# Two quarters of logits in one visit to TensorE, and reloads moved by one or two half products

## The chip, the cores and the metric

The kernel runs on one core of a Trainium2 chip. TensorE (PE in the profile, PEld its weight loads) multiplies matrices into PSUM. VectorE (DVE), ScalarE (ACT) and GpSimd (POOL) work element by element. The DMAs of this kernel are all issued by SyncE's queue (SP). The metric is the time of one execution on the device in microseconds, median of the runs.

## The reference, cut to what matters

Three layers follow one another: pooled attention (8 batches, 8 heads, 576 positions; keys and values averaged over 8 neighbours), a feed-forward layer on its 4608 tokens, and a soft mixture of experts on the result.

```python
x = attention(q, k, v)                  # 4608 tokens x 512
h = x @ w_in                            # 512 -> 2048, the first layer
g = maximum(h, 0) ** 2                  # 4608 x 2048
x2 = g @ w_out                          # 2048 -> 512
logits = x2 @ phi                       # 512 -> 32 slots
d = exp(logits - logits.max(0));  d /= d.sum(0)
slot_input = d.T @ x2                   # 32 x 512
slot_out = experts(slot_input)          # 8 experts, 512 -> 1024 -> 512
c = exp(logits - logits.max(1));  c /= c.sum(1)
return c @ slot_out
```

The kernel never forms x2. It multiplies w_out by phi once (a matrix A, 2048 x 32, tile `a_sb`) and takes the logits as g @ A. The sum d.T @ x2 is taken as (d.T @ g) @ w_out.

## The kernel before, in words

The tokens are 36 tiles of 128. The columns of h (d_ff, 2048) are four quarters j of 512. One product is one tile by one quarter: 12 matmuls (line 400; xh and xl are the high and the low part of the activations), so 144 products in all. Tiles 0 to 3 go by a list of their own; after that the pairs of tiles (t, t+1) follow one another, quarter by quarter. A slot is half a product, 6 matmuls; a table `ev` says what is issued after which slot, and a scheduler then sets the order on each engine. `issue_after` pins work behind a named instruction: behind the last store, the last square on VectorE, or (new) the last first-layer matmul.

Each product goes through ScalarE (relu, line 412) and VectorE or GpSimd (square, line 418; VectorE reads the product straight from PSUM) and is stored to DRAM (line 422). The product's PSUM tile `l` has two buffers, so product n+2 waits until the square (or relu) of product n has read its own.

The logits of a pair of tiles need g transposed. `reload_turned` (line 447) reads 2 tiles by one quarter back from DRAM with four DMAs of 128 KB, into one of five buffers (tiles `turned` and `tmp`). `g_T` (line 455) transposes it in 32 x 32 blocks on VectorE. `logits` (line 480) then does four matmuls of 32 columns each, side by side in the array, 256 tokens long. Quarters accumulate in the PSUM tile `pl` and ScalarE copies the sum out (line 494). For the early pairs (t below ND = 10, and two late tiles) each quarter has a PSUM tile of its own (`att`, two buffers, shared with the attention); ScalarE copies the first quarter and VectorE adds the other three (line 492).

When all four quarters are there, `log_T` (line 506) spreads the logits, VectorE takes the maximum, ScalarE the exponentials, VectorE transposes them (line 541, tile `d`), and `dg` (line 551) adds d.T @ g to a running sum. Attention of later tiles (lines 188 to 289) runs between the products: on TensorE lines 188, 204 and 281, on ScalarE and VectorE the rest. After the last tile (about 737 us) the experts and the last product follow.

Of the kernel before, what the change touches and what calls it, by code (L numbers as in the profile page):

```python
# [17 lines left out]
def kernel(  # L18
# [12 lines left out]
    nc = tc.nc  # L31
# [9 lines left out]
    NT = NTOK // P  # L41
    NPAIR = H // 2
    KD = DM // P
    NQ = 4
# [4 lines left out]
    SLOTS = 8  # L49
    NI = 4  # L50
    ND = 10
# [41 lines left out]
    def ps(name):  # L93
        return ps2.tile([P, 512], F32, tag=name, name=name)
# [229 lines left out]
    st_t, mark, n_st = {}, {}, [0]  # L324
# [35 lines left out]
    def natural(x):  # L360
        return x.rearrange("p (a c f) -> p c a f", a=4, f=32)
# [25 lines left out]
    hp_t, g_t, gT_t, L_t, dT_t, d_t, sc_d = {}, {}, {}, {}, {}, {}, {}  # L387
    pl_t = {}

    def l1_half(t, j, half):  # L390
        if half == 0:
            hp_t[t, j] = ps("l1")
        xh, xl = x_t[t]
        w = wq[j]
        steps = [
            (x[:, kk], w[:, hl, kk]) for kk in range(KD) for x, hl in ((xh, 0), (xh, 1), (xl, 0))
        ]
        n = len(steps) // 2
        for i in range(half * n, (half + 1) * n):
            nc.tensor.matmul(hp_t[t, j], steps[i][0], steps[i][1], start=(i == 0), stop=(i == 2 * n - 1))  # L400
        if half == 1:
            hp = hp_t.pop((t, j))
            if j == NQ - 1 and ND <= t < NT - 4:
                g = tmp[:, 6 + t % 2]
            elif j == NQ - 2 and t % 2 == 0 and ND <= t < NT - 4:
                g = tmp[:, 4 + t // 2 % 2]
            else:
                g = gp.tile([P, QF], F32, tag="g", name="g")
            r = p2.tile([P, QF], F32, tag="r", name="r")
            sq = "VVVPVPVV"[2 * j + t % 2]  # L410
            last_relu.append(
                nc.scalar.activation(out=r, in_=hp, func=AF.Relu, scale=1.0 / (R * R if sq == "V" else R))  # L412
            )
            dst, src, pre = g, r, hp if sq == "V" else r
            if t >= NT - 4:
                dst = natural(g)
                src, pre = (y.rearrange("p (c a f) -> p c a f", c=4, f=32) for y in (src, pre))
            m = eng[sq].tensor_tensor(out=dst, in0=pre, in1=src, op=ALU.mult)  # L418
            if sq == "V":
                mark["sq"] = m  # L420
            if t < NT - 4:
                mark["store"] = nc.sync.dma_start(out=g_dram[t // 2][j, t % 2 * P:(t % 2 + 1) * P], in_=g)
            if t >= ND:
                g_t[t, j] = g
# [42 lines left out]
    def logits(t, j):  # L467
        gT = gT_t.pop((t, j))
        if (t, j) in gT_at:
            gT_free.append(gT_at.pop((t, j)))  # L470
        alone = t < ND or t in (NT - 4, NT - 2)
        n = P if t >= NT - 4 else 2 * P
        if alone:
            pl = ps("att")[:, :n]
        elif j == 0:
            pl = pl_t[t] = ps1.tile([P, n], F32, tag="pl", name="pl")
        else:
            pl = pl_t[t]
        for c in range(CPQ):
            mark["logits"] = nc.tensor.matmul(  # L480
                pl[32 * c:32 * c + 32],
                a_sb[:, c, 32 * j:32 * j + 32],
                gT[:, c],
                start=(alone or j == 0),
                stop=(alone or j == NQ - 1),
            )
        first = t - t % width(t)
        if first not in L_t:
            L_t[first] = p2.tile([P, 2 * P], F32, tag="plsb", name="plsb")
        dst = L_t[first][:, (t - first) * P:(t - first) * P + n]  # L490
        if alone and j > 0:
            nc.vector.tensor_tensor(out=dst, in0=dst, in1=pl, op=ALU.add)
        elif alone or j == NQ - 1:
            nc.scalar.copy(out=dst, in_=pl)

    run, order = {}, []

    def width(t):
        return 1 if t >= NT - 2 else 2
# [98 lines left out]
    def behind(names, fn, *a):  # L598
        with ExitStack() as es:
            for n in names:  # L600
                es.enter_context(tc.issue_after(mark[n].ins))
            fn(*a)
# [81 lines left out]
    def at(slot, fn, *a):  # L684
        ev.setdefault(slot, []).append((fn, a))
# [5 lines left out]
    def run_slot(s):  # L691
        for fn, a in ev.pop(s, []):
            if fn in (g_T, logits, log_T, d_T, dg) and a[0] >= NT - EP:
                early(fn, *a)
            else:
                fn(*a)
# [3 lines left out]
            fn(*a)  # L700

    def post(t, s0, o, step=4):
        for j in range(NQ):
            at(s0 + step * j + o[1], logits, t, j)
        for j in range(NQ):
            at(s0 + step * j + o[0], pinned, "sq", g_T, t, j)
            at(s0 + step * j + o[2], pinned, "store", reload_turned, t, j)

    def post_end(t, s0, p):
        at(s0 + p[0], log_T, t)  # L710
        at(s0 + p[1], d_T, t)
        at(s0 + p[2], dg, t)
# [34 lines left out]
    for j in range(NQ):  # L747
        s0 = 26 + 12 * j
# [7 lines left out]
        attention(t, a_at[t])  # L756
    for t in range(ND, NT - 2, 2):
        if t < NT - 4:
            post(t, SLOTS * t, (12, 14, 6))
        post_end(t, SLOTS * t, (27, 28, 28))  # L760
    for t in (NT - 4, NT - 2):
        s0 = SLOTS * t
        for i in range(2):
            for j in range(NQ):
                at(s0 + 4 * j + 2 * i + LO, logits, t + i, j)
            for j in range(NQ):
                at(s0 + 4 * j + 2 * i + GO, g_T, t + i, j)
# [8 lines left out]
    for t in range(0, ND, 2):  # L776
        s0 = 96 + 28 * (t // 2)
        at(s0 - 5, reload_g, t)
        post(t, s0, (1, 4, -4), 4)
        post_end(t, s0, (20, 21, 22))  # L780
    for b in range(1, B):
        s0 = a_at[b * S // P]
# [59 lines left out]
    steps = (att_qT, att_sc, att_exp, att_norm, att_aT, att_av)  # L842
# [14 lines left out]
    for u, (t, j) in enumerate(units):  # L857
        for half in range(2):
            l1_half(t, j, half)
            run_slot(2 * u + half)  # L860
        if j == NQ - 1:
            x_t.pop(t)
# [26 lines left out]
    for c in range(CPQ):  # L889
        for j in range(NQ):  # L890
# [4 lines left out]
                start=(c == 0),  # L895
                stop=(c == CPQ - 1),
# [12 lines left out]
    for r in range(NR):  # L909
        ph = [ps("l1") for _ in range(2)]  # L910
        for kk in range(KD):
            for n in range(2):
                for j in range(4):
# [4 lines left out]
                        start=(kk == 0),  # L918
                        stop=(kk == KD - 1),
# [104 lines left out]
```

## Time and profile before

| | |
|---|---|
| runs before | 822.71, 829.86, 825.0 us; median 825.0 |
| the profiled execution | 822.68 us, its span 820.7 us |
| TensorE busy | 762.3 us, 93% of the span |
| VectorE busy | 533.4 us, 65% |
| ScalarE busy | 373.2 us, 45% |
| GpSimd busy | 202.5 us, 25% |
| first logits | about 277 us |
| end of the last product's work | about 737 us |

A row of the profile's timeline has the start in us, the length in us, the engine, the line, the operation, the tile written, the tiles read, and in brackets how long the engine was idle before it and what released it. TensorE's float32 matmuls are recorded as two records each, so four logits matmuls read as x8. Starts, not ends, tell what a matmul costs, since matmuls overlap.

### The profile page before, as it was taken

The page shows a single profiled execution, that of the slowest core. Times are in us where ns is not written, and L with a number is a line of the kernel's source. Part 1 is how long each engine was busy: PE and PEld are TensorE (multiplying, and loading weights), DVE is VectorE, ACT ScalarE, POOL GpSimd, SP SyncE. Part 2 cuts the span into 40 slices and gives each one's busy share as a digit, 9 for nine tenths or more (in the row PEclk, how much of TensorE's full clock was granted, in tenths as well). Part 3 has the DMA queues.
Part 4 walks back from the last instruction along what each step waited for, and adds up shares of the span by engine and source line. Part 5 has one row for each costly group of instructions (what it writes and reads, how often), then busy time and mean ns, then how long its engine had stood idle before and what let it go on. Part 6 is the DMA issues. An engine that isn't in the chain of part 4 may idle for free.

```text
span 820.7 us, 14813 instructions
## 1 busy us (share of the span) xinstructions
PE 762.3 (93%) x5352; PEld 529.7 (65%) x5352; DVE 533.4 (65%) x1033; ACT 373.2 (45%) x1107; POOL 202.5 (25%) x208
## 2 busy tenths in 40 slices
PE   7699899979999999998999999979998999998993
PEld 6577678757677776665666666746665666663552
DVE  5886966577836687688868687876666564424333
ACT  3564456334456563453536464654365433331232
POOL 3433532149624330136024414301000001000000
PEclk8579999999999999999999999989999999999996
DMA  9755742666724885788598788667456424969999
GB/s 277 244 166 153 221 167 103 215 175 225 259 112 146 225 233 160 204 234 211 179 291 216 207 258 215 182 194 217 129 184 198 141 91 150 350 253 315 372 352 313
DMA packets 180856, 175.11 MB, mean 213 GB/s; under 512 B 47152, under 2 KB 138288, under 8 KB 180784
## 3 DMA queue, kind: packets, MB, share of 16 engines
q1 hardware_dynamic: 180784, 174.17, 67.9%
q8 instruction: 43, 0.70, 0.3%
q14 instruction: 29, 0.24, 0.1%
HBM read 126.94 MB, written 47.19 MB: 212 GB/s over the span
## 4 chain that ended last, share of the span: by engine, by line
PE 63%; DVE 15%; DMA 11%; ACT 6%; issue 3%; POOL 1%; SPq 1%; DVEq 0%; ACTq 0%
PE l L400 35%; DMA kv<-in_v_dram 3%; PE misc L551 3%; PE pl L480 3%; PE misc L946 2%; PE gT L281 2%; PE gT L204 2%; PE l L914 2%; PE att L281 2%; ACT aT L254 2%; PE att L204 2%; DVE vp L161 2%; DMA g_back<-g_dram 2%; ACT es L215 1%; PE att L480 1%
## 5 line engine op out<-in xcount | busy, mean ns | idle before, releaser
L400 PE MATMUL l<-w,xh 128*128 128x512 f32 x1152 | 383.5, 413 | 11.7 <-DVE g L418 7.0
L400 PEld LDWEIGHTS l<-w,xh 128*128 128x128 f32 x1152 | 209.4, 191 | 82.0 <-issue 17.7
L400 PE MATMUL l<-w,xl 128*128 128x512 f32 x576 | 230.9, 401 | 0.0
L412 ACT ACTIVATE r<-l 128x512 f32<-128x512 f32 x144 | 86.4, 601 | 185.5 <-PE l L400 168.8
L400 PEld LDWEIGHTS l<-w,xl 128*128 128x128 f32 x576 | 109.4, 190 | 30.1 <-issue 4.7
L418 POOL TENSOR_TENSOR g<-r 128x512 f32<-128x512 f32 x36 | 41.2, 1145 | 298.4 <-ACT r L412 247.4
L254 ACT COPY aT<-turned 32x256 f32<-32x256 f32 (+1 forms) x168 | 67.8, 404 | 33.6 <-DVE turned L263 31.3
L418 DVE TENSOR_TENSOR g<-l,r 128x512 f32<-128x512 f32 x75 | 51.2, 684 | 47.2 <-ACT r L412 40.9
L131 POOL TENSOR_TENSOR kv<-kv 72x512 f32<-72x512 f32 x40 | 53.8, 1348 | 88.0 <-DMA kv<-in_v_dram 59.5
L455 DVE STREAM_TRANSPOSE turned<-turned 128x1024 f32<-128x1024 f32 x39 | 47.7, 1230 | 3.8 <-DMA turned<-g_dram 3.7
L256 DVE COPY aT<-turned 32x256 f32<-32x256 f32 (+1 forms) x120 | 43.7, 365 | 5.0 <-PE gT L281 3.1
L317 POOL TENSOR_TENSOR tmp<-tmp 128x512 f32<-128x512 f32 x21 | 28.6, 1361 | 68.8 <-DVE tmp L314 68.8
L215 ACT ACTIVATE es<-att,mx 128x72 f32<-128x72 f32 x120 | 36.8, 333 | 16.2 <-DVE mx L211 16.0
L215 ACT ACTIVATE es<-gT,mx 128x72 f32<-128x72 f32 x120 | 36.8, 329 | 12.7 <-DVE mx L211 12.6
L350 POOL TENSOR_TENSOR w<-tmp,w 128x512 fp32r<-128x512 f32 x16 | 28.6, 1793 | 38.5 <-ACT w L349 34.2
L418 DVE TENSOR_TENSOR tmp<-l,r 128x512 f32<-128x512 f32 x33 | 22.6, 686 | 21.2 <-ACT r L412 15.1
L551 PE MATMUL misc<-g,d 128*32 128x512 f32 x134 | 25.8, 631 | 7.3 <-DVE d L541 7.3
L455 DVE STREAM_TRANSPOSE tmp<-tmp 128x1024 f32<-128x1024 f32 x25 | 30.7, 1231 | 2.4 <-DMA tmp<-g_dram 2.4
L238 DVE TENSOR_TENSOR es<-es,rs 128x576 f32<-128x576 f32 x36 | 31.6, 878 | 1.0
L307 DVE TENSOR_SCALAR tmp<-tmp 128x512 uint32<-128x512 uint32 x32 | 20.0, 624 | 17.4 <-ACT tmp L306 17.4
L132 POOL TENSOR_TENSOR kv<-kv 72x256 f32<-72x256 f32 x40 | 30.3, 763 | 0.6
L204 PEld LDWEIGHTS gT<-kb,qT 128*128 128x128 f32 (+1 forms) x176 | 23.4, 188 | 8.2 <-issue 5.1
(188 smaller groups left out, 1135.3 us busy)
## 6 DMA issues: line engine op xcount, KB each, us to landing
g_dram<-g SPq DMA_DIRECT2D x95, 256.0 KB
turned<-g_dram SPq DMA_DIRECT2D x156, 128.0 KB
w<-in_moe_w_dram SPq DMA_DIRECT2D x32, 512.0 KB
tmp<-g_dram SPq DMA_DIRECT2D x100, 128.0 KB
w<-in_moe_w_dram SPq DMA_DIRECT2D x6, 2048.0 KB
g_back<-g_dram SPq DMA_DIRECT2D x10, 1024.0 KB
kv<-in_k_dram SPq DMA_DIRECT2D x32, 288.0 KB
kv<-in_v_dram SPq DMA_DIRECT2D x32, 288.0 KB
```

The costliest lines, as they stand in the source:

```text
L131: eng.tensor_tensor(out=x[:, :, 0:4], in0=x[:, :, 0:4], in1=x[:, :, 4:8], op=ALU.add)
L204: nc.tensor.matmul(sc[off:off + n, i * 2 * SP:(i + 1) * 2 * SP], qT[:, pi, off:off + n], kb[b % 2][:, pi].rearrange("p a s -> p (a s)"),)
L215: nc.scalar.activation(out=es[:, e], in_=sv[:, h], func=AF.Exp, bias=mx[:, e:e + 1], accum_out=rsum[:, t % 8, e, 0:1],)
L254: nc.scalar.copy(out=dst, in_=src)
L256: eng[e].tensor_copy(dst, src)
L281: nc.tensor.matmul(px[e * D:(e + 1) * D, i * P + off:i * P + off + n], vp_t[b][:, 2 * i + e], aT[:, 2 * i + e, off:off + n],)
L400: nc.tensor.matmul(hp_t[t, j], steps[i][0], steps[i][1], start=(i == 0), stop=(i == 2 * n - 1))
L412: nc.scalar.activation(out=r, in_=hp, func=AF.Relu, scale=1.0 / (R * R if sq == "V" else R))
L418: m = eng[sq].tensor_tensor(out=dst, in0=pre, in1=src, op=ALU.mult)
L455: nc.vector.transpose(out=gc.rearrange("p (n i) -> p n i", i=32), in_=gc.rearrange("p (n f) -> p n f", f=32))
L480: mark["logits"] = nc.tensor.matmul(pl[32 * c:32 * c + 32], a_sb[:, c, 32 * j:32 * j + 32], gT[:, c], start=(alone or j == 0), stop=(alone ...
L551: mark["dg"] = nc.tensor.matmul(dp[32 * j:32 * j + 32], d[:, u], g if t < NT - 4 else natural(g), start=(u == 0), stop=(u == width(t) - 1),)
```

## The change

Logits of two quarters are issued together (`logits_two`), each pinned behind the latest first-layer matmul. For the early pairs the first two quarters share one PSUM tile `att`, and the last two share another: one copy on ScalarE and one addition on VectorE in place of one copy and three additions. The transposes and reloads of even quarters are moved by two slots more than those of odd ones. In slots from the start of the pair, the transposes of the four quarters were at 12, 16, 20, 24 and are now at 14, 16, 22, 24; the reloads were at 6, 10, 14, 18 and are now at 9, 11, 17, 19; the logits were at 14, 18, 22, 26 and are now at 18 and 26 for two each. For the early pairs: transposes 1, 5, 9, 13, now 4, 6, 12, 14; reloads -4, 0, 4, 8, now 0, 2, 8, 10; logits 4, 8, 12, 16, now 8 and 16.

```diff
-            nc.tensor.matmul(hp_t[t, j], steps[i][0], steps[i][1], start=(i == 0), stop=(i == 2 * n - 1))
+            mark["l1"] = nc.tensor.matmul(hp_t[t, j], steps[i][0], steps[i][1], start=(i == 0), stop=(i == 2 * n - 1))
...
-        alone = t < ND or t in (NT - 4, NT - 2)
+        alone = t in (NT - 4, NT - 2)
+        two = t < ND
...
+        elif two and j % 2 == 0:
+            pl = pl_t[t] = ps("att")[:, :n]
...
-                start=(alone or j == 0),
-                stop=(alone or j == NQ - 1),
+                start=(alone or j == 0 or two and j == 2),
+                stop=(alone or j == NQ - 1 or two and j == 1),
...
-        if alone and j > 0:
+        if alone and j > 0 or two and j == 3:
             nc.vector.tensor_tensor(out=dst, in0=dst, in1=pl, op=ALU.add)
-        elif alone or j == NQ - 1:
+        elif alone or j == NQ - 1 or two and j == 1:
             nc.scalar.copy(out=dst, in_=pl)
+
+    def logits_two(t, j):
+        behind(["l1"], logits, t, j - 1)
+        behind(["l1"], logits, t, j)
...
     def post(t, s0, o, step=4):
+        for j in (1, 3):
+            at(s0 + step * j + o[1], logits_two, t, j)
         for j in range(NQ):
-            at(s0 + step * j + o[1], logits, t, j)
-        for j in range(NQ):
-            at(s0 + step * j + o[0], pinned, "sq", g_T, t, j)
-            at(s0 + step * j + o[2], pinned, "store", reload_turned, t, j)
+            b = s0 + step * j + (0 if j % 2 else 2)
+            at(b + o[0], pinned, "sq", g_T, t, j)
+            at(b + o[2], pinned, "store", reload_turned, t, j)
...
-            post(t, SLOTS * t, (12, 14, 6))
+            post(t, SLOTS * t, (12, 14, 7))
...
-        post(t, s0, (1, 4, -4), 4)
+        post(t, s0, (2, 4, -2), 4)
```

What it does to the order shows at two places. The first is TensorE around products 68 and 69 (`l_3617` and `l_3655` before, `l_3602` and `l_3638` in the change). Before:

```order
L400 MATMUL l_3617<-w_577,xh 128x512 x2
L480 MATMUL att<-turned,a_sb 32x256 x4
L400 MATMUL l_3617<-w_577,xl 128x512
L400 MATMUL l_3617<-w_577,xh 128x512 x2
L400 MATMUL l_3617<-w_577,xl 128x512
L400 MATMUL l_3655<-w_577,xh 128x512 x2
L400 MATMUL l_3655<-w_577,xl 128x512
L400 MATMUL l_3655<-w_577,xh 128x512 x2
L400 MATMUL l_3655<-w_577,xl 128x512
L480 MATMUL pl<-tmp,a_sb 32x256 x4
L400 MATMUL l_3655<-w_577,xh 128x512 x2
```

The same place in the change (line 483 is line 480 of before):

```order
L281 MATMUL gT<-aT,vp 64x128 x8
L400 MATMUL l_3638<-w_577,xh 128x512 x2
L400 MATMUL l_3638<-w_577,xl 128x512
L400 MATMUL l_3638<-w_577,xh 128x512 x2
L400 MATMUL l_3638<-w_577,xl 128x512
L483 MATMUL pl<-turned,a_sb 32x256 x4
L483 MATMUL pl<-tmp,a_sb 32x256 x4
L400 MATMUL l_3638<-w_577,xh 128x512 x2
```

Two groups of four logits matmuls that stood apart now stand together between two halves of a product.

The second place is SyncE's queue around the stores of products 63 to 66 (line 422; `g_dram_104` belongs to an early pair, `g_dram_110` to the pair just computed). Before:

```order
L422 DMA g_dram_110<-tmp 128x512
L447 DMA turned<-g_dram_110 32x8x128 x4
L422 DMA g_dram_110<-tmp 128x512
L447 DMA turned<-g_dram_104 32x8x128 x4
L114 DMA qt<-in_q_dram 128x8x64
L422 DMA g_dram_111<-g 128x512
L447 DMA tmp<-g_dram_110 32x8x128 x4
L124 DMA kv<-in_v_dram 72x2x512 x2
L124 DMA kv<-in_k_dram 72x2x512
L422 DMA g_dram_111<-g 128x512
L447 DMA tmp<-g_dram_104 32x8x128 x4
```

In the change:

```order
L422 DMA g_dram_110<-tmp 128x512
L124 DMA kv<-in_v_dram 72x2x512
L422 DMA g_dram_111<-g 128x512
L447 DMA turned<-g_dram_110 32x8x128 x4
L124 DMA kv<-in_v_dram 72x2x512
L124 DMA kv<-in_k_dram 72x2x512
L422 DMA g_dram_111<-g 128x512
L447 DMA tmp<-g_dram_110 32x8x128 x4
L447 DMA turned<-g_dram_104 32x8x128 x4
L422 DMA g_dram_111<-g 128x512
```

The reloads stand behind later stores, and some stand two in a row.

## Rows read from the trace of the kernel before

**Rows 1.** The page's first part: engine, busy us (share of the span) xinstructions.

```profile
span 820.7 us, 14813 instructions
PE 762.3 (93%) x5352; PEld 529.7 (65%) x5352; DVE 533.4 (65%) x1033; ACT 373.2 (45%) x1107; POOL 202.5 (25%) x208
```

**Rows 2.** Tile pl, matmuls and copies: ns min/median/max, first and last start.

```profile
L480 PE MATMUL pl<-turned,a_sb x216: 378/379/404, 276.9 to 679.0; 128*32 128x256 f32 x108
...
L494 ACT COPY plsb<-pl x13: 254/373/415, 304.2 to 737.6; 128x256 f32<-128x256 f32 x11, 128x128 f32<-128x128 f32 x2
```

**Rows 3.** Windows: us, busy PE PEld DVE ACT POOL, clock, DMA share, GB/s.

```profile
350.00:450.00 100.00, 95.96 (x639) 63.86 (x632) 78.48 (x147) 48.75 (x162) 33.31 (x39) 1.00 0.82 228
...
500.00:550.00 50.00, 44.77 (x287) 28.98 (x280) 38.36 (x82) 28.90 (x98) 15.17 (x20) 0.93 0.67 191
```

**Rows 4.** Timeline of TensorE's weight loads, the longest idle stretches from 277 us.

```profile
379.55 0.30 PEld L400 LDWEIGHTS l<-w,xh 128*128 128x128 f32 x2 [3.72 <-DVE tmp L418]
...
544.51 0.18 PEld L551 LDWEIGHTS misc<-g,d 128*32 128x32 f32 x3 [4.72 <-issue]
...
548.11 0.50 PEld L400 LDWEIGHTS l<-w,xh 128*128 128x128 f32 x2 [1.66 <-DVE tmp L418]
...
629.40 0.42 PEld L188 LDWEIGHTS att<-ident,qt 128*128 128x128 f32 x4 [2.64 <-issue]
```

**Rows 5.** Timeline of TensorE, one group of logits between first-layer matmuls.

```profile
397.96 0.39 PE L400 MATMUL l<-w,xl 128*128 128x512 f32 x1
...
398.66 0.40 PE L400 MATMUL l<-w,xl 128*128 128x512 f32 x1
398.99 0.64 PE L480 MATMUL pl<-turned,a_sb 128*32 128x256 f32 x8
...
400.13 0.39 PE L400 MATMUL l<-w,xl 128*128 128x512 f32 x1
```

**Rows 6.** Timeline of TensorE, two groups of logits in a row.

```profile
301.18 0.40 PE L400 MATMUL l<-w,xl 128*128 128x512 f32 x1
...
301.96 0.61 PE L480 MATMUL pl<-turned,a_sb 128*32 128x256 f32 x8
...
303.08 0.40 PE L400 MATMUL l<-w,xl 128*128 128x512 f32 x1
```

**Rows 7.** Line 492: its instructions, and VectorE's idle us before them, times.

```profile
L492 DVE TENSOR_TENSOR plsb<-plsb,att x21: 277/404/421, 305.2 to 735.6; 128x256 f32<-128x256 f32 x15, 128x128 f32<-128x128 f32 x6
...
  PE att L480: 13.9, 9
```

**Rows 8.** Timelines of SyncE's queue and VectorE: reloads and their transposes, a busy case.

```profile
364.19 1.96 SPq L447 DMA_DIRECT2D tmp<-g_dram  x4
...
370.05 1.25 DVE L455 STREAM_TRANSPOSE tmp<-tmp 128x1024 f32<-128x1024 f32 x1 [1.10 <-DMA tmp<-g_dram]
```

**Rows 9.** The same timelines, a quiet case.

```profile
602.99 1.87 SPq L447 DMA_DIRECT2D turned<-g_dram  x4
...
607.21 1.25 DVE L455 STREAM_TRANSPOSE turned<-turned 128x1024 f32<-128x1024 f32 x1
```

**Rows 10.** Line 455: VectorE's idle us before the transposes, times, by releaser.

```profile
  DMA turned<-g_dram: 3.7, 3
  DMA tmp<-g_dram: 2.4, 2
```

**Rows 11.** Chain that ended last, in order of time: start us, us, what.

```profile
365.70 4.23 DMA tmp<-g_dram
...
378.81 0.70 DVE tmp L418
379.55 3.06 PE l L400 x12
```

**Rows 12.** Timelines of TensorE and VectorE: `log_T` and the last transposes to `d`.

```profile
688.49 0.70 PE L506 MATMUL misc<-plsb,s4rep 128*128 128x256 f32 x2
...
691.88 0.74 DVE L541 STREAM_TRANSPOSE d<-dT 32x64 f32<-32x64 f32 x3
```

## The prediction

> **What bounds the kernel now.** I read the page's first part: TensorE is busy 93% of the span, no other engine above 65% [rows 1]. A busy TensorE is not one at its peak, so the stage has to be looked at. The tile of the logits places it: the first logits start at 276.9 us, the last copy of their sums at 737.6 us [rows 2]. By the order before the change 47.5 of the 144 products stand ahead of the first logits, so 96.5 products take 460.7 us, 4.8 us each. Nothing ahead of 276.9 us moves on TensorE, and after 737.6 us the work is the same. The windows say what sets the pace: from 350 to 450 us TensorE is busy 95.96 of 100 us, VectorE 78.48, and the DMA engines have a share of 0.82 [rows 3]. TensorE bounds, with VectorE and the DMA close enough to stop it at single places. The idle stretches before weight loads name these: 3.72, 4.72, 1.66 and 2.64 us, 12.7 us together [rows 4]. Two of them end with the square of a product on VectorE, so what makes VectorE late ends in TensorE's time.
>
> **A. Fewer visits of the logits to TensorE.** One group of logits between first-layer matmuls: from the xl matmul at 398.66 to the next one at 400.13 is 1.47 us; undisturbed the step is 398.66 - 397.96 = 0.70; the visit costs 0.77 [rows 5]. Two groups in a row: 303.08 - 301.18 - 0.70 = 1.20 [rows 6]. So the second group costs 0.43, and each merging saves 0.77 - 0.43 = 0.34 us. There are 32 pairs of quarters, but the scheduler does not keep them all together. In the order before, TensorE leaves the first layer 124 times from product 47 on, in the change 114 times. Of the visits that hold logits of the tiles up to 31 there are 58 before (6 of them with two whole groups) and 46 after (17 with two). 10 fewer visits make 10 x 0.34 = -3.4 us; 12 would make -4.1. The matmuls are as many as before. The saving lies on the engine that bounds. Its other end is 0: if TensorE only comes earlier to a wait for VectorE, nothing is left. I take -3.4.
>
> **B. Ten additions fewer on VectorE.** The five early pairs had 15 of the 21 additions of line 492 and keep 5. Ten at the median 0.404 make 4.0 us of VectorE's time, and VectorE idled 13.9 us in front of such additions, behind logits that TensorE had not reached [rows 7]; some of that goes too. ScalarE's copies of the early pairs stay five. VectorE is not the bound, so most of this lies beside TensorE's work; it counts only where a square was late. Ends: 0 and -4. I take -1, nearer to 0, since only two of the four stretches ended with VectorE's square [rows 4].
>
> **C. Reloads closer to their transposes.** Reloads and transposes both move to later slots, the reloads by more. Counted by squares of products on VectorE between the store that a reload stands behind on SyncE's queue and its transpose, 42 of the 64 reloads had three, 22 had two, none one. In the change 2 have three, 47 have two, 15 have one. The mean falls from 2.67 to 1.83, by 0.84 x 4.8 = 4.0 us. Each reload is four DMAs: issuing takes 1.9 us, and the transpose began 607.21 - 604.86 = 2.35 us after the last issue in a quiet stretch, without a wait for it [rows 9], and 370.05 - 366.15 = 3.9 us after it in a busy one, having waited 1.10 for it [rows 8]. With the store ahead in the queue that is 4.5 to 6.5 us from a square to landed data. Two products leave 9.6 us, which covers it. One leaves 4.8 us and what VectorE does first, in several cases another transpose of 1.25 us [rows 8]: about even in quiet stretches, late by one to two in busy ones. Behind a late transpose VectorE's whole queue stands: squares, additions, attention. Before, late data cost VectorE 3.7 + 2.4 = 6.1 us in five waits [rows 10]. What one can cost TensorE shows in the chain: the reload that landed at 369.9 led through VectorE's queue to the square at 378.81 and the 3.72 us stretch [rows 4, 11]. If the waits double, one more such stretch comes: +3.7. Some relief stands against it: reloads of third quarters no longer stand one store behind their own data, and the early pairs' first reload leaves later than the 2 MB of `g_back` that stood just ahead of it. Ends: 0, and four stretches, +14.9. I take +3, near the one stretch for five waits that the trace has.
>
> By the row a reload is late within 3.9 us of its last issue. The Trainium skill, page "DMA: Bandwidth & Descriptors", section "Anatomy of one DMA", gives about 2.0 us fixed plus the bytes at 436 GB/s, measured for DMAs of another queue; for 128 KB an estimate by that page is 2.3 us. The quiet case agrees with it, the busy one does not; by the page term C would be 0 and the sum 3 us lower. Its section "Latency and other measured facts" puts memory latency ten times higher under load, which speaks against shortening the lead where the DMA share is 0.82; the trace agrees in direction, 3.9 against 2.35 us. I keep the row.
>
> **D. Distance from `log_T` to `dg`.** The shortest chain runs from 688.49 to 691.88 + 0.74 = 692.62: 4.1 us from the matmul to the last transpose [rows 12]. TensorE needs that much other work between the two. Where the order had none, at 540 us, it stood for 4.72 us [rows 4]. In the change some distances shrink: around product 55 twelve first-layer matmuls and two of q by k remain, 12 x 0.233 + 0.45 = 3.3 us (the 0.233 is a third of the 0.70 [rows 5]; the 0.45 is estimated by the 0.43 of a group of logits), where 5.0 stood by the same count; around product 63 about 4.0 for 6.5. At product 104 the empty place gets two more matmuls, about 1 us. So +0.8, about +0.5 for several near the edge, -1 at 104, and more where VectorE is busy and the chain longer. Ends: -3 (the place at 104 clears far enough) and +5. I take +1.5.
>
> **Edits at nothing.** GpSimd's and ScalarE's queues issue no DMA and keep their work; that the logits wait for a first-layer matmul holds back only TensorE's own order; the shared PSUM tile `att` is asked for ten times fewer, held longer by one group, 0.43 us.
>
> **The sum.** -3.4 - 1 + 3 + 1.5 = +0.1. On the profiled execution, 822.7 us, that is 822.8. The median of the runs, 825.0, stands 2.3 above it; three runs spread over 7 us, so I go halfway less a little: **823.5 us**.
>
> **Rivals.**
> *Late reloads bind VectorE (slower).* Place: the 15 reloads with one square between them and their transpose, and the two-square ones from 350 to 450 us. For it: five late ones with much more lead [rows 10], VectorE at 78% there [rows 3]. Against it: elsewhere the DMA share is lower, and a late transpose costs nothing while no product waits. It decides once four or more of them reach a waiting product, 4 x 3.72 = 14.9 in place of C's 3: 823.5 + 11.9 = 835 us.
> *The idle stretches go (faster).* They hang on single places of the order, which is now another. If those of 3.72, 4.72 and 1.66 us go [rows 4], with half of what the clock lost there (0.93 granted from 500 to 550 us, a mean of 2.4 GHz and, after the engine had stood still, 1.2 GHz: 0.07 x 50 = 3.5 us [rows 3]) and term C, 823.5 - 10.1 - 1.8 - 3 = 809 us; with two of the three about 812. For it: B and the added work at product 104. Against it: nothing in the change aims at them, and C pulls the other way.
> *The change does not do what it says.* Only 17 of 32 pairs stay together, and 29 visits still hold one group. If the saving is then eaten by the next wait, A is 0 and the time 823.5 + 3.4 = 827 us.
>
> **How the numbers follow.** Forecast 0.57, late reloads 0.16, stretches gone 0.14, A lost 0.13. About 1% is what a measurement of this kernel can tell from no change: 816.8 to 833.3 us. Forecast and lost A lie within. So faster 0.14, same 0.70, slower 0.16. The range reaches from the two-of-three case, 812, to just short of the late reloads, 834; beyond lies about a fifth. It holds the ends of A, B and D, and of C up to three stretches.
>
> **What will show it.** A: visits of two groups cost about 1.2 us between xl matmuls, and logits loads have fewer idle gaps. B: 11 additions of line 495 and less idle time before them. C: VectorE's idle time before line 455 for DMA, 6.1 us before; 12 confirms, 25 or more is the first rival. D: idle time of TensorE before `dg` about product 55 and 63. I am wrong if TensorE's idle stretches differ by more than 8 us from the 12.7 shown, or if anything ahead of 277 or after 738 us changes its length.

## The result, and the profile after

The change makes the kernel slower: 829.9 us median of 20 runs (821.8 to 835.9) against 824.5 us for the kernel before in 20 runs beside it, a ratio of 1.0056 with a 95% interval of 1.0029 to 1.0083. The forecast was 823.5 us. The time lies inside the range and inside the class "within 1%", but the difference, some 4.6 us by the ratio, is more than the measurement's uncertainty, and the sum of the terms had come out at +0.1. (The ratio is of the fast runs alone, and three of the change's 20 were slow, so it says a little less than the two medians, which are 5.4 us apart.)

The page's first part after the change, to be held against [rows 1]:

```profile
span 826.3 us, 14795 instructions
PE 760.6 (92%) x5352; PEld 530.5 (64%) x5352; DVE 527.0 (64%) x1023; ACT 374.1 (45%) x1107; POOL 202.5 (25%) x208
```

No engine is busy for more than 1 us longer than before, TensorE and VectorE are busy for less, and the span is 5.6 us longer. So no engine got more work; something stands still. Where, the answer for line 455 (the transposes that read the reloads) tells: VectorE's idle time before them, with the number of times, and below it who waited for them, to be held against [rows 10]:

```profile
  DMA tmp<-g_dram: 24.5, 8
  DMA turned<-g_dram: 10.3, 8
...
  PEld pl L483: 5.0, 1
  PE pl L483: 4.5, 1
  PEld att L483: 0.9, 1
```

VectorE now idles 34.8 us in 16 waits for a reload to land, where it was 6.1 us in five. Some of it reaches TensorE: the logits' matmuls (line 483 now, 480 before) wait behind the transposes. Before the change no weight load waited more than 0.4 us for line 455 directly. Most of the 34.8 us falls while TensorE has other work. Two places do not. The first is near 294 us: the row of SyncE's queue, VectorE's rows, then TensorE's weight load (start, duration, engine, line, operation, and in brackets the idle time ahead with what ended it):

```profile
287.26 5.30 SPq L447 DMA_DIRECT2D tmp<-g_dram  x8
...
294.25 1.25 DVE L455 STREAM_TRANSPOSE tmp<-tmp 128x1024 f32<-128x1024 f32 x1 [5.53 <-DMA tmp<-g_dram]
295.93 1.25 DVE L455 STREAM_TRANSPOSE tmp<-tmp 128x1024 f32<-128x1024 f32 x1 [0.43 <-DMA tmp<-g_dram]
...
297.24 0.19 PEld L483 LDWEIGHTS att<-tmp,a_sb 128*32 128x32 f32 x8 [2.84 <-issue]
```

Two reloads stand in a row here, and their eight DMAs take 5.30 us to issue. VectorE waits 5.53 us for the first and 0.43 us for the second. TensorE's weight load starts 0.06 us after the second transpose ends (295.93 + 1.25), so it is the second reload that holds it up. That one landed 3.4 us after its last issue (295.93 - 292.56), and 9.1 us after the store ahead of the two, at 286.87: it is late by its place in the queue, behind another reload.

The second is near 377 us. SyncE's queue first, then VectorE, then TensorE's weight loads:

```profile
366.15 0.37 SPq L124 DMA_DIRECT2D kv<-in_v_dram  x1
366.62 0.33 SPq L124 DMA_DIRECT2D kv<-in_k_dram  x1
367.05 0.35 SPq L422 DMA_DIRECT2D g_dram<-g  x1
367.49 3.29 SPq L447 DMA_DIRECT2D tmp<-g_dram  x4
370.88 4.65 SPq L447 DMA_DIRECT2D turned<-g_dram  x4
...
377.22 1.25 DVE L455 STREAM_TRANSPOSE tmp<-tmp 128x1024 f32<-128x1024 f32 x1 [4.35 <-DMA tmp<-g_dram]
...
373.37 0.16 PEld L483 LDWEIGHTS pl<-turned,a_sb 128*32 128x32 f32 x8 [0.36 <-issue]
378.52 0.20 PEld L483 LDWEIGHTS pl<-tmp,a_sb 128*32 128x32 f32 x8 [4.99 <-DVE tmp L455]
...
380.13 0.33 PEld L400 LDWEIGHTS l<-w,xl 128*128 128x128 f32 x1
380.55 0.76 PEld L400 LDWEIGHTS l<-w,xh 128*128 128x128 f32 x2
```

Read it from the top. Two loads of keys and values and a store are issued, then the four DMAs of the reload, which take 3.29 us to issue instead of 1.9 [rows 9]. The last is issued at 370.78; the transpose that waited for the data starts at 377.22, so they land 6.4 us after the last issue and 10.2 us after the store ahead of them. The prediction had 2.35 us (quiet) and 3.9 us (busy) from the last issue [rows 8, 9], and 4.5 to 6.5 us in all. (The Trainium skill, page "DMA: Bandwidth & Descriptors", section "Anatomy of one DMA", gives about 2.0 us fixed plus bytes over bandwidth, by which I estimated 2.3 us; the measured 6.4 us decides here.) TensorE had done the first of the pair's two groups at 373.37 and stands 4.99 us before the second. And the stop costs more than itself: the two weight loads of the first layer that take 0.42 us at full clock take 0.76 after it, the single one 0.33 in place of 0.19 (the rows at full clock are those of a_aside, below).

The windows show both places and the whole stretch from the 41st product's first weight load to the 137th's (us; busy PE, PEld, DVE, ACT, POOL; granted clock, DMA share, GB/s):

```profile
276.01:314.59 38.58, 35.06 (x218) 24.43 (x216) 23.78 (x47) 19.39 (x63) 10.85 (x11) 0.96 0.74 201
...
354.19:395.21 41.02, 36.51 (x228) 24.66 (x226) 28.20 (x51) 15.92 (x46) 20.39 (x23) 0.92 0.74 192
...
247.63:704.95 457.32, 437.26 (x2769) 299.46 (x2768) 314.50 (x648) 223.21 (x696) 96.35 (x109) 0.98 0.65 192
```

The same stretch before the change, between the same two products:

```profile
250.07:700.38 450.31, 436.28 (x2769) 295.06 (x2769) 319.74 (x658) 222.85 (x696) 94.16 (x109) 0.99 0.66 195
```

The stretch is 7.0 us longer. TensorE's busy time grew by 1.0 us of it and its idle time by 6.0; the granted clock fell from 0.99 to 0.98 of 2.4 GHz, and in the two places it was 0.96 and 0.92: TensorE ran at 1.2 GHz for a part of these windows, after it had stood still. Ahead of the stretch, where TensorE's order is that of before, the profiled execution of the change was 2.4 us quicker, and behind it 1.0 us slower, which is why the spans differ by 5.6.

### The profile page after: what moved, and what is told of

Same layout as the page of the kernel before. It is cut to its first block, busy times and chain, and to the rows that moved or that the text cites. A ratio compares the mean times of both kernels' runs of the same rounds, so it can differ in the third digit from the quotient of the medians.

```text
span 826.3 us, 14795 instructions
## 1 busy us (share of the span) xinstructions
PE 760.6 (92%) x5352; PEld 530.5 (64%) x5352; DVE 527.0 (64%) x1023; ACT 374.1 (45%) x1107; POOL 202.5 (25%) x208
## 5 line engine op out<-in xcount | busy, mean ns | idle before, releaser
L256 DVE COPY aT<-turned 32x256 f32<-32x256 f32 (+1 forms) x120 | 41.4, 345 | 3.3 <-PE gT L281 1.6
L215 ACT ACTIVATE es<-gT,mx 128x72 f32<-128x72 f32 x120 | 36.7, 327 | 10.5 <-DVE mx L211 10.4
L350 POOL TENSOR_TENSOR w<-tmp,w 128x512 fp32r<-128x512 f32 x16 | 26.7, 1678 | 38.1 <-ACT w L349 33.8
```

The lines of the kernel that those rows point to most:

```text
L215: nc.scalar.activation(out=es[:, e], in_=sv[:, h], func=AF.Exp, bias=mx[:, e:e + 1], accum_out=rsum[:, t % 8, e, 0:1],)
L256: eng[e].tensor_copy(dst, src)
```

## The experiments

Two theories. **Late reloads**: the shorter way from reload to transpose makes VectorE wait, and at some places TensorE behind it. **Order**: the change sorts the instructions anew (the slots are inputs of a scheduler), and any new order may be better or worse by half a per cent. A third, that the pairing itself costs time, was tested as well. All ratios are to the kernel before, run beside them, with the 95% interval; each set had five rounds on one chip, and the three sets were on three chips. "Base" is the slot of the first early tile's work, `s0`.

### First set: give the lead back, take the pairing back

The change with the reloads one slot earlier. At base 96 that needs a sixth reload buffer, so the early tiles move to base 95 or 99:

```
-            post(t, SLOTS * t, (12, 14, 7))
+            post(t, SLOTS * t, (12, 14, 6))
-        s0 = 96 + 28 * (t // 2)
+        s0 = 95 + 28 * (t // 2)      # lead_99: 99
-        post(t, s0, (2, 4, -2), 4)
+        post(t, s0, (2, 4, -3), 4)
```

> The change with its pairs kept, the reloads one slot earlier (main 7 to 6, early -2 to -3, and the early pairs one slot earlier so that five buffers suffice). By the order, 49 reloads have three squares between their store and their transpose, 15 two, none one (mean 2.77, the change 1.83). Late reloads are the cause: VectorE waits under 10 us for DMA before the transposes (30.6 in the change), the time 1.0% below the change, 820 to 823 us. The pairing itself is the cause (logits stand on TensorE for two transposes): 829 to 832 us as in the change, with the wait before the transposes gone. Chance of the order: 820 to 835 whatever the DMA waits are.

> The same with the early pairs three slots later in place of one earlier: another order on every engine, the same lead (49 reloads with three squares, 15 with two). Late reloads are the cause: under 10 us of DMA waits before the transposes and 820 to 824 us, like its twin. The pairing: 829 to 832 us. Chance of the order: it differs from its twin by as much as from the change.

Measured: 820.1 us, 0.9996 (0.9963 to 1.0028), and 817.5 us, 0.995 (0.9922 to 0.9979). VectorE's waits fell to 8.1 us and, in lead_99, to 5.6 us in four (34.8 in the change, not the 30.6 of the expectation). The kernel before took 821.1 us on this chip, 3 us less than in the first measurement, so times in us stand that much lower than the expectations of this set. The twins are 0.46% apart, nearly as much as lead_95 is from the change, which was the sign named for the order.

Then the kernel before, unpaired, with its reloads one slot later, and the change with pairing and bank sharing taken back but its short lead kept:

```
 # b_late1, in the kernel before
-            post(t, SLOTS * t, (12, 14, 6))
+            post(t, SLOTS * t, (12, 14, 7))
-        post(t, s0, (1, 4, -4), 4)
+        post(t, s0, (1, 4, -3), 4)
 # a_apart, in the change
-        alone = t in (NT - 4, NT - 2)
-        two = t < ND
+        alone = t < ND or t in (NT - 4, NT - 2)
+        two = False
-        for j in (1, 3):
-            at(s0 + step * j + o[1], logits_two, t, j)
+        for j in range(NQ):
+            at(s0 + step * j + o[1] + (0 if j % 2 else 2), logits, t, j)
```

> The kernel before with nothing paired, its reloads alone one slot later (main 6 to 7, early -4 to -3): 42 reloads with two squares, 21 with one, one with three (mean 1.69). Late reloads are the cause: 25 to 40 us of DMA waits before the transposes and 829 to 834 us. The pairing is the cause: 825 us as before.

> The change with its transposes and reloads where they are, but each quarter's logits issued by themselves two slots after its transpose, unpinned, one bank each for the early pairs: pairing and bank sharing taken back, the short lead kept (47 reloads with two squares, 14 with one). Late reloads are the cause: 25 us or more of DMA waits, 830 to 835 us (the change plus the 3 us that its merged visits save). The pairing is the cause: 823 to 826 us.

Measured: b_late1 826.8 us, 1.0055 (1.0026 to 1.0083), with 35.7 us of waits in 21; a_apart 837.3 us, 1.0169 (1.0119 to 1.0219). In b_late1 line 455's answer has

```profile
  DMA turned<-g_dram: 18.4, 12
  DMA tmp<-g_dram: 17.3, 9
...
  PEld pl L480: 2.8, 4
```

So the later reloads, put into the old kernel without anything else, cost what the whole change cost, with about the same waits. The pairing does not look like the cause: a_apart, without it and with the short lead, is 1.1% slower than the change. But it has six runs, and its waits, 19.8 us, stayed under the 25 expected, so what makes it slower still is not shown. And this set moved the early tiles together with the lead, and the order with every edit.

### Second set: the controls

shift_95 and shift_99 are the change with its short lead and only the base moved; a_late1 shortens the lead once more ((12, 14, 8) and (2, 4, -1)); a_nopin calls the two logits without the pin behind a first-layer matmul.

```
-        s0 = 96 + 28 * (t // 2)
+        s0 = 99 + 28 * (t // 2)      # shift_95: 95
 # a_nopin
-        behind(["l1"], logits, t, j - 1)
-        behind(["l1"], logits, t, j)
+        logits(t, j - 1)
+        logits(t, j)
```

> The change with its short lead kept (products between the reload's request and the transposes that read it: 47 times two, 15 once one, mean 1.80, as in the change) and only the early tiles' work moved three products later, as in lead_99. Late reloads (theory): VectorE's waits for a reload's DMA before the transposes of line 455 stay at 20 us or more (34.8 us in the change, 5.6 us in lead_99), time over before 1.003 to 1.012, so slower than lead_99's 0.995 by about 1%. Rival, the place of the early tiles in the order did it: waits may stay, but the ratio comes out at 0.992 to 0.999 as with lead_99.

> The change with its short lead kept (47 times two, 14 one, 3 three, mean 1.83) and only the early tiles' work moved one product earlier, as in lead_95. Late reloads: DMA waits before the transposes 20 us or more (lead_95 had 8.1 us), ratio over before 1.003 to 1.012 against lead_95's 0.9996. Rival, the order of the early tiles did it: ratio 0.997 to 1.002 whatever the waits are.

> The change with each reload asked for one slot later still (products between request and transposes: 34 times two, 23 one, 4 none, 3 three, mean 1.56 against 1.83). Late reloads: VectorE's DMA waits before the transposes grow from 34.8 us to 45 to 70 us, more of them reach TensorE, ratio over before 1.010 to 1.020. Rival, the lead is hidden and the change's 1.0056 has another cause: ratio 1.003 to 1.008, with no longer stretch of TensorE that ends on line 455.

> The change without the pin that holds the two quarters' logits behind a first-layer matmul; their slots stay, the scheduler places them (52 visits with logits and 115 in all from the stage on, against 46 and 114 by the pin; lead of the reloads as in the change, 47 two, 14 one, 3 three). Theory: the pin's own worth is some 6 visits with logits at 0.34 us, 0 to 2 us, and the DMA waits stay near 35 us, so the ratio is 1.004 to 1.012. Rival, the pin makes TensorE wait for the transposes (logits placed before their tile is ready) and is what costs the time: ratio 0.998 to 1.002 and DMA waits that no longer reach TensorE.

Measured: shift_99 813.0 us, 0.990 (0.9866 to 0.9933); shift_95 826.4 us, 1.0044 (1.0007 to 1.0081); a_late1 823.3 us, 1.0021 (0.9988 to 1.0054); a_nopin 825.5 us, 1.0041 (1.0001 to 1.008). Only shift_95 came out as late reloads had it (a_nopin did in its ratio, but waited 23.3 us where some 35 were expected). With the same short lead shift_99 is 1% faster than before, and a_late1, whose lead is shorter still, is not slower than the change. In a_late1 the waits did not grow, 28.0 us in 17; in shift_99 they were

```profile
  DMA turned<-g_dram: 8.6, 5
  DMA tmp<-g_dram: 7.7, 4
...
  PEld l L400: 1.0, 4
  PEld pl L483: 0.4, 1
```

and none of them stopped TensorE for more than 1.0 us in sum. So the lead, counted in products, does not give the waits, and the waits do not give the time: it matters where a wait falls. The order could even be the whole story. What was missing was an experiment that takes the waits away and leaves the order alone. The pin is worth nothing that these runs can tell.

### Third set: the waits away, the order kept

In a_aside and b_aside most reloads are issued as before, with the same bytes, but into a scratch area in DRAM; the transposes use what the buffer holds. SyncE's queue keeps its order but for a few places. In a_aside the reloads whose removal would have changed TensorE's order keep their buffer (six, and three more are first fills of a buffer), so TensorE and ScalarE run the change's own order.

```
         gc = gT_t[t, j] = turned()[i]
+        if filled[i] and (t, j) in ASIDE:      # b_aside: if filled[i]
+            gc = dram.tile([P, 2 * QF], F32, tag=f"aside{t}_{j}", name=f"aside{t}_{j}")
+        filled[i] = 1
         for c in range(CPQ):
             nc.sync.dma_start(
```

> The change with the reloads taken out of the transposes' way: 55 of the 64 reloads are asked for at the same places and move the same bytes, but write to a scratch area in DRAM, and VectorE's transposes work on what the SBUF buffer already holds (so the results of early and main tiles' logits are not the reference's). TensorE's and ScalarE's order of instructions is the change's, row by row; VectorE's differs in 10 of 1025 rows. Late reloads (theory): VectorE's 34.8 us of DMA waits before the transposes fall to 5 to 8 us, the two stretches of TensorE behind them (2.84 us at 297, 4.99 us at 378) go, and the ratio over before falls from the change's 1.0056 to 0.996 to 1.001. Rival, the change's order of work costs the time whether the reloads are late or not: ratio 1.004 to 1.008.

> The kernel before with 59 of its 64 reloads written to a scratch area in DRAM in the same way (logits of early and main tiles not the reference's); the orders of TensorE, VectorE and ScalarE are exactly those of before. Its DMA waits before the transposes were 6.1 us and one of them stood behind the 3.72 us stretch at 379.55. Late reloads: 2 to 4 us faster than before, ratio 0.995 to 0.998, so that with a_aside at 0.996 to 1.001 the rest of the change is worth about nothing. Rival: sending the reloads to DRAM speeds up something else (the stores, the loads, the clock), and the ratio falls below 0.992 here too, so that a_aside proves nothing.

Measured: a_aside 818.3 us, 0.9946 (0.991 to 0.9982), with 5.7 us of waits left; b_aside 817.2 us, 0.9944 (0.9913 to 0.9976), with none. Both fell a little further than expected; b_aside stayed short of the 0.992 that would have spoiled the comparison. Without the waits the two kernels take the same time: over 12 runs each their means are 0.6 us apart, with a 95% interval of 2.6 us to either side. With them the change takes 1.0056 and the kernel before 1. So sending the reloads aside is worth 1.1%, about 9 us, to the change, and 0.56%, about 4.6 us, to the kernel before, which is more than its 6.1 us of waits were expected to cost; what else it changes was not measured, but it is done to both. The difference, 4.5 us, is as large as the whole loss. It is good to some 3.5 us: the loss of 4.6 is known to 2.2, the equality of the pair to 2.6, and the 1.0056 is from another set than the pair.

The traces show where. a_aside's windows between the same products as the change's two places, and its whole stretch:

```profile
278.92:313.52 34.60, 33.51 (x217) 23.52 (x215) 25.51 (x47) 19.28 (x63) 10.59 (x11) 1.00 0.78 224
352.76:387.40 34.64, 34.64 (x231) 23.78 (x230) 26.86 (x52) 16.01 (x46) 18.35 (x20) 1.00 0.77 225
250.50:694.68 444.18, 431.77 (x2768) 297.01 (x2768) 314.74 (x647) 223.13 (x695) 96.02 (x109) 1.00 0.65 197
```

The first place takes 34.60 us for 38.58, the second 34.64 for 41.02, each with the clock back at 1.00. That is 10.4 us for idle stretches of 2.84 and 4.99: TensorE's idle time in the two windows is 6.9 us less without the waits, and its busy time, at the higher clock, 3.4 us less. The weight loads at the second place, TensorE's order being the same, now stand without a stop:

```profile
372.30 0.16 PEld L488 LDWEIGHTS pl<-turned,a_sb 128*32 128x32 f32 x8 [0.36 <-issue]
372.55 0.35 PEld L488 LDWEIGHTS pl<-tmp,a_sb 128*32 128x32 f32 x8
...
373.64 0.19 PEld L400 LDWEIGHTS l<-w,xl 128*128 128x128 f32 x1
373.88 0.42 PEld L400 LDWEIGHTS l<-w,xh 128*128 128x128 f32 x2
```

b_aside's stretch between the same products is

```profile
248.19:695.48 447.29, 435.82 (x2769) 294.25 (x2769) 319.54 (x658) 222.87 (x696) 95.36 (x109) 0.99 0.64 196
```

so in these profiles the waits cost the change 457.32 - 444.18 = 13.1 us there and the kernel before 450.31 - 447.29 = 3.0. Of the 13.1 us the two places hold 10.4; the other 14 waits leave at most 2.7.

The last two: the kernel before with only its base moved to 99, and the change at its own base with only the main tiles' reloads one slot earlier.

```
 # b_99, in the kernel before
-        s0 = 96 + 28 * (t // 2)
+        s0 = 99 + 28 * (t // 2)
 # r_6_2, in the change
-            post(t, SLOTS * t, (12, 14, 7))
+            post(t, SLOTS * t, (12, 14, 6))
```

> The kernel before, unpaired and with its own lead, with only the early tiles' work three products later (base 99 for 96). Theory after shift_99 (0.990) and lead_99 (0.995): the place of the early tiles in the order is worth 0.5 to 1.5% by itself, so 0.987 to 0.995 here. Rival, pairing needs that place, and the two together gave the 1%: ratio 0.997 to 1.004.

> The change at its own place (base 96) with only the main tiles' reloads asked for one slot earlier (products between request and transposes: 34 three, 25 two, 5 one, mean 2.45 against 1.83). Nine of the change's 16 DMA waits, 18.6 of 34.8 us, stood before main tiles' transposes. Late reloads: waits fall to 10 to 20 us, no stretch of TensorE ends on a main tile's transposes, ratio 0.997 to 1.003. Rival, the lead is not what costs: ratio 1.004 to 1.008.

Measured: b_99 821.4 us, 0.9968 (0.9939 to 0.9996), between the two expectations: the place of the early tiles alone brings at most a part of shift_99's 1%. (Nor is it the place alone: by the order the lead is 2.2 products and not that of before, as the expectation has it, and VectorE waited 32.2 us.) r_6_2 816.2 us, 0.9898 (0.9864 to 0.9932), more than expected, although VectorE still waited 23.1 us:

```profile
  DMA tmp<-g_dram: 18.2, 5
  DMA turned<-g_dram: 4.9, 3
...
  PEld l L400: 1.0, 2
  PEld pl L483: 0.4, 1
```

One number in the change's code, 7 to 6, takes 1.6% off it, and the two stretches with it. r_6_2 and shift_99 beat the kernel before by about 1%. r_6_2 is also 0.5% below a_aside, beside which it ran (interval 0.3% to either side): with waits it is faster than the change is without them. So its gain is not the lead's alone; its order is another too.

All kernels in one table. Lead: products between request and transposes, mean by the order. Waits: VectorE's for reloads, in the profiled execution. Stretch: from the 41st to the 137th product there.

| kernel | lead | waits, us | stretch, us | ratio |
|---|---|---|---|---|
| before | 2.67 | 6.1 | 450.3 | 1 |
| the change | 1.83 | 34.8 | 457.3 | 1.0056 |
| lead_95 | 2.77 | 8.1 | 454.2 | 0.9996 |
| lead_99 | 2.77 | 5.6 | 448.9 | 0.995 |
| shift_95 | 1.83 | 27.1 | 457.3 | 1.0044 |
| shift_99 | 1.80 | 16.3 | 440.9 | 0.990 |
| a_late1 | 1.56 | 28.0 | 452.7 | 1.0021 |
| a_nopin | 1.83 | 23.3 | 455.6 | 1.0041 |
| r_6_2 | 2.45 | 23.1 | 443.7 | 0.9898 |
| b_late1 | 1.69 | 35.7 | 454.8 | 1.0055 |
| a_apart | 1.83 | 19.8 | 464.5 | 1.0169 |
| b_99 | 2.2 | 32.2 | 453.1 | 0.9968 |
| a_aside | none | 5.7 | 444.2 | 0.9946 |
| b_aside | none | 0 | 447.3 | 0.9944 |

The stretch follows the ratio in the main; lead and waits do not (16.3 to 35.7 us of waits go with ratios from 0.990 to 1.0169). Where TensorE stands says more. The change's two stops, 2.84 us at 297 and 4.99 at 378, have their like in shift_95 (2.91 at 294, 4.52 at 369) and a_late1 (2.54 at 294, 4.04 at 373). r_6_2, shift_99, lead_99 and a_aside have no stop above 2.5 us ahead of 400 us. b_99 is the exception: stops of 4.87 and 4.12 us before the attention's matmuls, and yet 0.9968.

## Why the prediction was wrong, step by step

**A, fewer visits, -3.4: held in the main.** A visit of two groups, from the xl matmul at 400.36 to the next at 402.25, less the 0.70 of an undisturbed step, costs 1.19 us, against 1.20 forecast:

```profile
400.36 0.39 PE L400 MATMUL l<-w,xl 128*128 128x512 f32 x1
400.68 1.07 PE L483 MATMUL pl<-turned,a_sb 128*32 128x256 f32 x16
...
402.25 0.39 PE L400 MATMUL l<-w,xl 128*128 128x512 f32 x1
```

In the traces of the stretch TensorE leaves the first layer 109 times for 119, ten fewer as by the order. What that is worth shows best without the waits: TensorE is busy 431.77 us in a_aside's stretch and 435.82 in b_aside's, 4.1 us less. A part of this is the clock. These are the parts of the two stretches with half the clock, one of a_aside and then two of b_aside:

```profile
537.10:540.50 3.40, 3.40 (x20) 1.01 (x18) 3.27 (x8) 0.91 (x3) 0.00 (x0) 0.50 1.05 404
...
536.20:543.10 6.90, 3.08 (x16) 0.68 (x16) 6.62 (x21) 2.81 (x9) 0.00 (x0) 0.51 0.51 196
659.10:662.50 3.40, 3.40 (x18) 1.08 (x11) 1.47 (x4) 0.00 (x0) 0.00 (x0) 0.50 0.20 77
```

TensorE was busy in them for 3.4 and 6.5 us. Half of the difference, 1.5 us, is what the clock can make; some 2.5 us are left for A, an estimate from these rows. The medians of a_aside and b_aside neither show nor exclude it.

**B, ten additions fewer, -1: not separated.** The additions and the idle time before them fell, from 13.9 us in nine [rows 7] to

```profile
  PE att L483: 8.4, 4
```

while ScalarE's copies of the sums (line 497, 494 before) now wait more for the same logits:

```profile
  PE pl L483: 16.3, 8
  PE att L483: 3.8, 2
```

where these two were 4.2 us in two and 3.9 in three before. Part of the waiting changed engines; neither engine bounds.

**C, late reloads, +3: the step that failed.** The mechanism was right: a late reload, VectorE's queue behind it, TensorE behind VectorE. Its size was wrong, in two of its links. First, "4.5 to 6.5 us from a square to landed data. Two products leave 9.6 us, which covers it": at 367 us the way took 10.2 us from the store alone, and at 287 us, with two reloads in a row, 9.1. The busy row that I had priced it by stood behind a store and one load of queries; the reload at 367 us stands behind two loads of keys and values of 288 KB each, and the next reload is issued right behind it. The kernel before had such a case, which I overlooked. Behind three of these loads and the store at 353.31 came

```profile
353.75 2.57 SPq L447 DMA_DIRECT2D turned<-g_dram  x4
...
363.41 1.25 DVE L455 STREAM_TRANSPOSE turned<-turned 128x1024 f32<-128x1024 f32 x1 [1.86 <-DMA turned<-g_dram]
```

that is 7.1 us from the last issue and 10.1 from the store, which a longer lead hid but for 1.86 us. (That these neighbours make the difference is read from the rows of both kernels; no run changed them alone.) The waits did not double, they grew from 6.1 to 34.8 us, past the 25 that I had named for the rival. Second, "one more such stretch: +3.7": two came, and they cost 10.4 us, not 3.7 each, because the pair's second group holds up all of TensorE at the spot and the clock falls. By the aside pair C was 9.1 - 4.6 = +4.5 us by the medians, and 13.1 - 3.0 = +10 us in the profiled stretch. The prediction's end of four stretches, +14.9, covered it; my choice "near the one stretch for five waits" did not, because it took the mean price of waits that mostly fall beside other work. The rival's rule, four reloads that reach a waiting product, 835 us, was as wrong on the other side: two reached one, and the other 14 waits cost little.

**D, `log_T` to `dg`, +1.5: its stop came, its sum did not.** Product 55 has the forecast stop, and in a_aside it is there with the same length:

```profile
312.69 0.14 PEld L558 LDWEIGHTS misc<-g,d 128*32 128x32 f32 x3 [1.50 <-ACT r L412]
```

None was seen at product 63. But TensorE's idle time before `dg` fell. From 250 to 700 us, before the change and after it (count, busy us and mean ns, idle us before it and what ended that):

```profile
L551 PE MATMUL misc<-g,d 128*32 128x512 f32 x110 | 22.8, 638 | 7.0 <-DVE d L541 7.0
...
L558 PE MATMUL misc<-g,d 128*32 128x512 f32 x110 | 24.0, 666 | 4.9 <-DVE d L548 4.8
```

Without the waits it is 7.7 us in b_aside and 4.5 in a_aside. The 4.72 us before `dg` at product 104 [rows 4] went. Against it the attention's matmuls (lines 188, 204 and 281) wait 5.3 us for 3.2 in the same 450 us. So D alone came out at about -2 to -3 us, and at about nothing with the attention's waits, where +1.5 was forecast. The list of the longest stretches [rows 4] had also left one out, 1.89 us before `dg` at 665 us.

**The sum.** In the two profiled executions C explains the loss: of 6.0 us more idle time in the stretch, the logits have 7.3 where they had none, `dg` 2.1 less, the attention 2.1 more and the first layer 1.4 less. By the medians the miss is shared: C has +4.5 for +3, and A, B and D, forecast at -2.9 together, come out at 0.6 us, good to 2.6, by the aside pair. Which of the two holds is open, since a single execution of a kernel can lie anywhere in the 15 us over which the runs of the kernel before spread; in both C came out above +3, clearly in the profiles and within the noise by the medians. Of the signs that the prediction named, the idle time's 6.0 us stay short of the 8, and the parts ahead of and behind the stretch did change their length, by 2.4 and 1.0 us.

**The rivals.** That A was eaten is not excluded by the medians, though its saving shows in TensorE's busy time; the idle stretches did not go. Late reloads were the right rival with a third to two thirds of its price. The order, which none of the cases named, moves this kernel too: r_6_2 is 0.5% faster than a_aside, which has hardly a wait left. Of the 1.4% between shift_99 and shift_95, which differ in nothing but a base, a part may be the waits, since shift_95 has the two stops and shift_99 neither. Why base 99 takes short leads without harm, and what of the 0.7% between b_99 (0.9968) and shift_99 (0.990) is the pairing's, stays open. That the waits cost the change what it lost is shown by the aside pair; r_6_2 agrees, but gained more than the waits can account for.

## What to carry to other kernels

Price a shorter lead by the worst place that it can fall on, with the DMAs that will stand ahead of it and behind it in the queue, and not by the mean over waits that other work hid; the kernel before may have shown such a place already, as it did at 353 us. The sum of an engine's waits says little: follow each to the bounding engine and add what the clock costs after a stop. To tell a lost wait from a lucky order, take the wait away while the bounding engine's instructions keep their order, in the kernel before and in the changed one.

## What the runs showed of the hardware

A reload of four 128 KB DMAs landed 2.35 us after its last issue in a quiet place [rows 9], 3.9 in a busy one [rows 8], 6.4 behind two loads of keys and values in the change, and 7.1 behind three in the kernel before. At 367 us the issuing itself took 3.29 us for four, and 4.65 for the four after them, against 1.9. After stops of 2.84 and 4.99 us TensorE ran its next weight loads at half speed (0.76 us for 0.42; granted clock 0.96 and 0.92 in the two windows, 1.00 in a_aside's), and the two windows cost 10.4 us for 7.8 us of idle time.
